# Fixing every engine's order by a table, splitting the first matmul groups by contraction halves, pairing k-v products and moving casts to ScalarE in a fused attention and feed-forward kernel

## The chip, the cores and the metric

The kernel runs on one core of one Trainium2 chip. The metric is device time in microseconds (us) of one execution, lower is better. The profile's span is about 1.8 us shorter than that time (308.2 us of span for a run of 310.04 us before). Engines: PE = TensorE, DVE = VectorE, ACT = ScalarE, POOL = GpSimd, SP = SyncE.

## The reference, cut to what matters

```python
# attention without a sequence-by-sequence product: q, k, v are (8, 8, 576, 64)
q_s = softmax(q, axis=-1)                      # over the 64 channels
k_s = softmax(k, axis=2)                       # over the 576 positions
kv  = einsum('bhsd,bhse->bhde', k_s, v)        # a 64x64 matrix per head
attn = einsum('bhsd,bhde->bhse', q_s, kv)
# feed-forward on x = (4608, 512): 512 -> 2048 -> 512
h = x @ w_in
g = where(h > 0, h, exp(min(h, 0)) - 1)
out = g @ w_out
```

The kernel works in 16 units of attention (two per batch; a unit n is four heads of a batch) and nine blocks of 512 tokens of feed-forward. GEMM1 is `x @ w_in`, GEMM2 is `g @ w_out`; each is 576 matmuls of 128 x 128 weights by 512 columns in fp32r (4 bytes a number: W1's 512 x 2048 come in eight transfers of 512 KB). In a block GEMM1 has eight groups of eight matmuls, counted from 0. In the names of the profiles W is a weight, QR, KR and VR are the loaded q, k and v, QS is q divided by its sums, VB is v in bf16, MBLK is the scaled k-v product, XT is the attention's result X (the x of GEMM1), ESB is the activation's buffer, GT is g, PS is PSUM and OSB the buffer of a finished tile.

## The kernel before

All work is described as a list of operations with an engine, a modelled duration and the buffers read and written. A scheduler then walks the list with a model of the machine and picks, for each engine, what to issue next. Semaphore waits follow from the buffers.

```python
def order(self):                      # the kernel before
    seq = self.one_pass({})           # greedy: the earliest ready operation, ties by key
    for _ in range(8):
        seq = self.one_pass(self.fluid(seq))   # again with modelled DMA landings
    return self.fill(seq)             # dummy matmuls in PE's modelled gaps at the start
```

The start of the program, which the argument is mostly about:

```python
for n, t in ((0, "q"), (1, "q"), (0, "k"), (0, "v"), (1, "k"), (1, "v")):
    self.load(n, t, -40, "sp", ...)           # 590 KB each, on SP's queue
    if (n, t) == (0, "v"): gate = S.ops[-1]
for s in range(4):                            # W1 by quarters of its columns, on POOL's queue
    self.load_w1(s, -30, [gate] if s == 0 else ())
# ... exp(q), exp(k) on ACT; V to bf16 on POOL; q sums and q/sum (QS) on DVE;
# ... q transposed by PE (side 'tp'), k-v product (kv_mm), X = kv applied to q (ao_mm), X evicted (xt)
self.side(0, -3, self.kv_mm(1, 0))
S.spare_until = S.ops[-1]                     # dummy matmuls stop here
```

A group of GEMM1 (`hg`) and what its result goes through, and the store of a finished tile:

```python
for t in range(2):
    for kc in range(4):                       # all four contraction chunks of W1 and X
        e.matmul(P[:, t*512:(t+1)*512], W1[:, kc, ...], XT[:, kc, ...], start=(kc==0), stop=(kc==3))
# ACT: esb = exp(P);  DVE: esb = min(esb,1)-1;  DVE: GT = max(esb, P)
...
S.add("act", ..., lambda e: e.activation(osb, bank, AF.Copy))         # out_store
for x in range(2):
    S.add("sp", ..., lambda e: e.dma_start(rows[b, c], osb[x*64:(x+1)*64, :]))
```

The softmax here doesn't subtract the row's maximum and nothing guards it: scores larger than these inputs give would overflow.

Of the kernel before, what the change touches and what calls it, by code (L numbers as in the profile page):

```python
# [19 lines left out]
ISSUE = {"sp": 620, "act": 650, "gp": 760}  # L20


class Op:
    __slots__ = ("eng", "dur", "emit", "deps", "key", "idx", "start", "end",
                 "dma", "sem", "val", "clock", "nbytes", "follow", "side", "late", "packet", "margin",
                 "gate")

    def __init__(self, eng, dur, emit, key, dma=None, nbytes=0):
        self.eng, self.dur, self.emit, self.key = eng, dur, emit, key
        self.deps = {}  # L30
        self.dma, self.nbytes = dma, nbytes
        self.start = self.end = None
        self.follow, self.side, self.packet, self.margin = None, 0, 4608, 0


class Sched:
# [3 lines left out]
    HOP = 90  # L40
    SLACK = 60
    LATE = 200
    SPIN_FROM = 3000.0
    DMA_LAT = 1650
    FIRST = {"sp": 1650, "act": 1650, "gp": 2300}
    DMA_RATE = 375.0
# [37 lines left out]
    def order(self):  # L84
        seq = self.one_pass({})
        for _ in range(8):
            seq = self.one_pass(self.fluid(seq))
        return self.fill(seq)

    def fill(self, seq):  # L90

        out, free, done = [], self.SPIN_FROM, False
        for o in seq:
            if o.eng == "pe" and not done:
                idle = o.start - free - 150
                count = int(36 + (idle - 3600) / 57 if free == self.SPIN_FROM else idle / 57)
                if count > 0:
                    p = Op("pe", count * 57, self.spare(count), 0)
                    p.start, p.end = free, free + p.dur
                    p.deps = {d: "raw" for d in self.spare_after}  # L100
                    out.append(p)
                free = o.end
                done = o is self.spare_until
            out.append(o)
        return out

    def fluid(self, seq):

        queues = {}
        for o in seq:  # L110
            if o.dma:
                queues.setdefault(o.eng, []).append([o.start + self.FIRST[o.eng], float(o.nbytes), o])
        t, land = 0.0, {}
        while any(queues.values()):
            live = [q[0] for q in queues.values() if q and q[0][0] <= t]
            coming = [q[0][0] for q in queues.values() if q and q[0][0] > t]
            if not live:
                t = min(coming)
                continue
            share = {id(x): self.DMA_RATE * x[2].packet / sum(y[2].packet for y in live)  # L120
                     for x in live}
            step = min([x[1] / share[id(x)] for x in live] + [c - t for c in coming])
            t += step
            for x in live:
                x[1] -= share[id(x)] * step
                if x[1] < 1:
                    land[x[2]] = t + 200 + x[2].margin
            for e in queues:
                queues[e] = [x for x in queues[e] if x[2] not in land]
        return land  # L130

    def one_pass(self, land):
        for o in self.ops:
            o.start = o.end = None
        queues = {e: [o for o in self.ops if o.eng == e] for e in self.ENG}
        free = {e: 0.0 for e in self.ENG}
        out, used = [], [0, -1, -2]
        left = len(self.ops)

        def ready(o):  # L140
            t = 0.0
            if o.follow is not None and o.follow.start is None:
                return None
            if o.gate is not None:
                if o.gate.start is None:
                    return None
                t = o.gate.start
            for d in o.deps:
                if d.end is None:
                    return None  # L150
                hop = self.HOP if d.eng != o.eng or d.dma else 0 if o.eng == "pe" else 40
                t = max(t, d.end + hop)
            return t

        while left:
            best = None
            for e in self.ENG:
                q = queues[e]
                if not q:
                    continue  # L160
                heads = q
                if e == "pe":
                    heads = [next((o for o in q if o.side == x), None) for x in (0, 1, 2)]
                    heads = [o for o in heads if o is not None]
                can = []
                for o in heads:
                    t = ready(o)
                    if t is not None:
                        if e == "pe" and o.side and o.late:
                            t += self.LATE  # L170
                        order = (used[o.side], o.idx) if e == "pe" else (o.key, o.idx)
                        can.append((max(t, free[e]), order, o))
                if not can:
                    continue
                first = min(c[0] for c in can)
                slack = 60 if e == "pe" else self.SLACK
                s, _, o = min((c for c in can if c[0] <= first + slack), key=lambda c: c[1])
                pick = (None, o, s)
                if pick and (best is None or pick[2] < best[2]):
                    best = (e, pick[1], pick[2])  # L180
            e, o, s = best
            queues[e].remove(o)
            if e == "pe":
                used[o.side] = s
            o.start = s
            free[e] = s + o.dur
            o.end = s + o.dur
            if o.dma:
                o.end = max(s + self.DMA_LAT + o.nbytes / self.DMA_RATE, land.get(o, 0))
            out.append(o)  # L190
            left -= 1
# [52 lines left out]
def t_act(n, psum):  # L244
    return n / 1.2 + (90 if psum else 105)


def t_dve(n, fast=1):
    return n / 0.96 / fast + 75


def t_f32r(n):
    return (n + 33) / 2.4


class Gen:
# [49 lines left out]
    def init(self):  # L306
# [4 lines left out]
            pattern=[[-1, 128]], channel_multiplier=1), -38, X=["ID"])  # L311
        S.add("dve", 60, lambda e: e.memset(self.RZK[0][:, :], 0.0), -90, W=["RZK0"])
        S.add("act", 1400, lambda e: e.activation(self.RZK[0][:, :], self.RZK[0][:, :], AF.Exp), -80,
              X=["RZK0"])
        for i in range(2):
# [5 lines left out]
    def load(self, n, t, key, eng="gp", follow=None):  # L321
# [9 lines left out]
        S.ops[-1].margin = 300 if n < 4 else 1500 if n < 6 else 5000  # L331
# [9 lines left out]
    def load_w1(self, s, key, after=()):  # L341
        w = self.w_in.rearrange("(h kc d) f -> h d kc f", h=2, d=D)
        sl = slice(s * 512, (s + 1) * 512)
        for h in range(2):
            self.S.add("gp", ISSUE["gp"], lambda e, h=h: e.dma_start(
                self.W1[h:128:2, :, sl], w[h, :, :, sl]), key,
                W=[f"W1_{s}{h}"], dma=f"w1{s}{h}", nbytes=1 << 19, after=after, follow=self.gpq)
            self.gpq = self.S.ops[-1]
        return self.gpq
# [9 lines left out]
    def stage1(self, n, key, vconv="gp"):  # L359
# [5 lines left out]
        S.add("act", t_act(1152, False), lambda e: e.activation(flat(q), flat(q), AF.Exp),  # L365
              key - 3, X=[f"qR{i}"])
        ek = self.ek(i)
        S.add("act", t_act(1152, False), lambda e: e.activation(  # L368
            ek[:, :, :, :].rearrange("p h c d -> p (h c d)"), flat(k), AF.Exp),
            key - 2, X=[f"kR{i}"])  # L370
        hs = slice(0, 2) if vconv == "gp" else slice(0, 1)
        eng, t = ("gp", 1250) if vconv == "gp" else ("dve", t_dve(576) + 60)
        S.add(eng, t, lambda e: e.tensor_copy(  # L373
            VB[:, hs, :, 0:D], v[:, hs, :, :]), key - 50, R=[vname], W=[f"VB{i}"])
        self.conv = S.ops[-1]
        if vconv != "gp":
            S.add("act", t_act(576, False), lambda e: e.activation(
                VB[:, 1:2, :, 0:D], v[:, 1:2, :, :], AF.Copy), key - 50, R=[vname],
                W=[f"VB{i}x"])
            self.conv2 = S.ops[-1]  # L380
        S.add("dve", t_dve(1152) + 60, lambda e: e.tensor_reduce(  # L381
# [3 lines left out]
        S.add("dve", 250, lambda e: e.reciprocal(self.RZQ[i][:, :, :], self.ZQ[i][:, :, :]),  # L385
# [3 lines left out]
        S.add("dve", t_dve(1152) + 60, lambda e: e.tensor_tensor(  # L389
# [8 lines left out]
    def tp(self, n, ps, key, engs=("act", "act"), after=()):  # L398
# [7 lines left out]
        for (c0, c1, at, X, W), eng in zip(cuts, engs):  # L406
# [7 lines left out]
            S.add("pe", (c1 - c0) * 56 + 60, mm, key, R=[f"QS{self.alt(n)}", "ID"], X=X, side=1)  # L414
# [6 lines left out]
            else:  # L421
                S.add("dve", t_dve(n_) + 60, lambda e, dst=dst, src=src: e.tensor_copy(dst, src),
                      key, W=W, X=X, after=after)

    def turn(self, n, key):

        i, qs = n % 2, self.QS[self.alt(n)]
        self.S.add("sp", ISSUE["sp"], lambda e: e.dma_start_transpose(
            self.QT[:, :, :], qs[:, :, :].rearrange("p c t -> p (c t)")),
            key - 60, R=[f"QS{self.alt(n)}"], W=["QT"], dma="tq", nbytes=128 * 2304)  # L430
        self.S.ops[-1].packet, self.S.ops[-1].margin = 512, 5000

    def widen(self, n, key):
        i, T = n % 2, self.qsT[self.alt(n)]
        self.S.add("gp", 1200, lambda e: e.tensor_copy(  # L435
            T[:, :, :].rearrange("p c t -> p (c t)"),
            self.QT[:, :, :].rearrange("p c t -> p (c t)")),
# [378 lines left out]
```

## Time and profile before

Three runs before the prediction had a median of 308.61 us (307.98 to 308.88). What matters:

| quantity | value | read from |
|---|---|---|
| 512-column matmuls | 1152, 1.81 us per eight, 261.2 us | PE timeline |
| first GEMM1 matmul | 16.91 us | PE timeline |
| last matmul ends | 304.30 us | chain of waits |
| stalls between 38 and 82 us | about 3.9 us, an estimate | PE timeline, start to start |
| W1's first two transfers land | 15.30 and 16.66 us | the trace's landings |

From the page of the kernel before: the span, each engine's busy time, PE's granted clock in 40 slices, and the chain of work that ended last.

```profile
span 308.2 us, 4602 instructions
PE 296.4 (96%) x1938; PEld 241.9 (78%) x1938; DVE 201.6 (65%) x244; ACT 161.9 (53%) x190; POOL 55.3 (18%) x54
...
PEclk9979999999999999999999999999999999999999
...
PE 87%; DMA 4%; DVE 4%; ACT 2%; issue 1%; POOL 1%; SPq 0%
```

PE is the chain for 87% of the span, so a gain can only come from its gaps, its clock or less work for it. The one digit 7 in the clock row is a cold stretch. The windows view of the kernel before shows it: each row is a stretch in us, its length, each engine's busy us (with instructions), the granted clock, the DMA share and GB/s.

```profile
14.00:17.00 3.00, 1.49 (x31) 1.07 (x15) 1.83 (x6) 2.00 (x5) 3.00 (x6) 0.99 1.11 331
17.00:20.00 3.00, 3.00 (x7) 2.34 (x8) 0.00 (x0) 0.00 (x0) 3.00 (x5) 0.50 1.19 373
38.00:50.00 12.00, 11.29 (x132) 8.76 (x131) 7.64 (x12) 6.36 (x8) 5.05 (x8) 1.00 1.12 374
60.00:70.00 10.00, 8.20 (x76) 6.10 (x75) 9.66 (x15) 8.12 (x10) 1.15 (x1) 1.00 0.83 255
100.00:110.00 10.00, 10.00 (x80) 8.23 (x79) 8.79 (x11) 4.79 (x7) 2.47 (x2) 1.00 0.72 236
```

From 17 to 20 us PE is "busy" all the time at half the clock: busy time alone hides it. From 60 to 70 us PE is idle for 1.8 us while DVE and ACT are both over 80% busy. At 100 us PE has no gap left. The waits of PE in the kernel before (us in total, times, longest), without some that end before 16 us. Of the 2.2 us in the first line, 1.7 end at 9.08 us, at the start, and 0.55 at 39.62:

```profile
PE PS L412 <- DVE QS L389: 2.2, 2, 1.7
...
PE PS L545 <- DMA W<-in_moe_w_in_dram: 1.0, 1, 1.0
PE PS L545 <- DVE GT L573: 0.8, 1, 0.8
PE PS L545 <- DVE GT L567: 0.7, 2, 0.4
PE PS L491 <- ACT XT L513: 0.6, 1, 0.6
```

The timeline of the start (start us, length us, engine, line, operation, and what ended the idle time before it) shows who started when:

```profile
9.77 1.15 POOL L373 CAST VB<-VR 128x1152 bf16<-128x1152 f32 x1 [8.31 <-DMA VR<-in_v_dram]
10.62 1.51 DVE L389 TENSOR_TENSOR QS<-QR,RZQ 128x1152 f16<-128x1152 f32 x1
10.86 5.08 POOL L345 DMA_DIRECT2D W<-in_moe_w_in_dram  x8
```

POOL casts unit 0's V first and issues W1's transfers after it. And the end of the same kernel in the timeline:

```profile
304.32 0.60 ACT L600 ACTIVATE OSB<-PS 128x512 f32<-128x512 f32 x1 [3.03 <-PE PS L583]
304.94 1.11 SPq L609 DMA_DIRECT2D out_dram<-OSB  x2
```

After the last eviction SP issues two half stores one after the other.

### The profile page before, as it was taken

Reading aid. Unit: us, or ns where it says so; the run is one execution under the profiler, and the core shown is the slowest. Engines: PE = TensorE matmul, PEld = TensorE weight load, DVE = VectorE, ACT = ScalarE, POOL = GpSimd, SP = SyncE. Lnnn points to the kernel's source line nnn. Section 1 sums busy time; section 2 is a strip of 40 time slices with the busy share of each in tenths; the row PEclk is TensorE's granted clock in tenths of the full one; section 3 lists DMA queues with packets and bytes.
Section 4 is the critical chain, followed back from the end, with each engine's and each line's share of the span. In section 5 each row is a group of like instructions: output and inputs, shape, how many; then the busy total and the mean of one; then the engine's idle time right before and its main releaser. Section 6 shows DMA issues by size and latency. Waiting matters only on the chain.

```text
span 308.2 us, 4602 instructions
## 1 busy us (share of the span) xinstructions
PE 296.4 (96%) x1938; PEld 241.9 (78%) x1938; DVE 201.6 (65%) x244; ACT 161.9 (53%) x190; POOL 55.3 (18%) x54
## 2 busy tenths in 40 slices
PE   7789999989999999999999999999999999999994
PEld 7567777668788888888888888888888888888783
DVE  3927874798897959595959596866544445555500
ACT  4738756979685546464646463734343443333311
POOL 0790144111211115050404040301000000000000
PEclk9979999999999999999999999999999999999999
DMA  7999999887778766566665654031111221111122
GB/s 263 312 361 389 390 389 323 273 264 136 242 186 228 260 157 187 150 186 149 183 150 159 168 169 87 21 78 30 34 36 39 46 47 41 34 34 34 36 68 68
DMA packets 33429, 49.39 MB, mean 160 GB/s; under 512 B 13952, under 2 KB 13952, under 8 KB 33408
## 3 DMA queue, kind: packets, MB, share of 16 engines
q1 hardware_dynamic: 27392, 33.63, 39.7%
q0 software_dynamic: 6016, 15.47, 16.0%
q8 instruction: 15, 0.25, 0.3%
q14 instruction: 6, 0.05, 0.1%
HBM read 36.70 MB, written 9.44 MB: 150 GB/s over the span
## 4 chain that ended last, share of the span: by engine, by line
PE 87%; DMA 4%; DVE 4%; ACT 2%; issue 1%; POOL 1%; SPq 0%
PE PS L545 42%; PE PS L583 41%; DMA VR<-in_v_dram 2%; PE PS L491 2%; DMA W<-in_moe_w_in_dram 2%; PE PS L461 2%; DVE QS L389 1%; ACT ESB L554 1%; DVE ZQ L381 1%; DVE GT L567 1%; ACT ESB L565 1%; SPq L329 0%; DVE GT L573 0%; PE PS L412 0%; POOL VB L373 0%
## 5 line engine op out<-in xcount | busy, mean ns | idle before, releaser
L545 PE MATMUL PS<-XT,W 128*128 128x512 f32 x576 | 144.0, 394 | 2.5 <-DMA W<-in_moe_w_in_dram 1.0
L583 PE MATMUL PS<-W,GT 128*128 128x512 f32 x576 | 144.9, 393 | 0.0
L545 PEld LDWEIGHTS PS<-XT,W 128*128 128x128 f32 x576 | 108.6, 190 | 26.9 <-DVE GT L567 1.8
L554 ACT ACTIVATE ESB<-PS 128x1024 f32<-128x1024 f32 x72 | 73.9, 1027 | 95.3 <-PE PS L545 95.2
L583 PEld LDWEIGHTS PS<-W,GT 128*128 128x128 f32 x576 | 106.1, 188 | 22.0 <-DVE GT L573 0.5
L571 DVE TENSOR_SCALAR ESB<-ESB 128x1024 f32<-128x1024 f32 x64 | 52.0, 813 | 68.0 <-ACT ESB L554 67.6
L573 DVE TENSOR_TENSOR GT<-ESB,PS 128x1024 fp32r<-128x1024 f32 x64 | 78.1, 1221 | 2.2
L600 ACT ACTIVATE OSB<-PS 128x512 f32<-128x512 f32 x32 | 19.2, 599 | 35.1 <-PE PS L583 35.1
L435 POOL CAST qsT<-QT 128x1152 fp32r<-128x1152 f16 x10 | 18.4, 1843 | 95.6 <-PE PS L461 91.7
L373 POOL CAST VB<-VR 128x1152 bf16<-128x1152 f32 x15 | 20.0, 1335 | 56.2 <-DMA VR<-in_v_dram 56.2
L381 DVE TENSOR_REDUCE ZQ<-QR 128x18 f32<-128x1152 f32 x16 | 21.6, 1349 | 6.3 <-ACT QR L365 6.2
L389 DVE TENSOR_TENSOR QS<-QR,RZQ 128x1152 f16<-128x1152 f32 x16 | 23.6, 1477 | 0.5
L513 ACT ACTIVATE XT<-PS 128x640 fp32r<-128x640 f32 (+5 forms) x32 | 19.7, 618 | 3.0 <-PE PS L491 2.8
L365 ACT ACTIVATE QR<-QR 128x1152 f32<-128x1152 f32 x16 | 18.6, 1165 | 2.9 <-DMA QR<-in_q_dram 2.9
L368 ACT ACTIVATE KR<-KR 128x1152 bf16<-128x1152 f32 x16 | 18.6, 1161 | 1.6 <-DMA KR<-in_k_dram 1.6
L491 PE MATMUL PS<-qsT,MBLK 128*128 128x320 f32 (+3 forms) x64 | 14.2, 306 | 1.1 <-ACT XT L513 0.6
L491 PEld LDWEIGHTS PS<-qsT,MBLK 128*128 128x128 f32 x64 | 11.6, 189 | 4.5 <-DVE MBLK L474 1.0
L567 DVE SCALAR_TENSOR_TENSOR GT<-PS,ESB 128x1024 fp32r<-128x1024 f32 x8 | 9.8, 1222 | 6.0 <-ACT ESB L565 6.0
L474 DVE TENSOR_TENSOR MBLK<-PS,RZK 64x128 fp32r<-64x128 f32 x32 | 9.3, 289 | 1.1
L648 PE MATMUL PS<-ID 128*128 128x128 f16 x92 | 8.4, 269 | 1.5 <-POOL ID L309 1.5
L648 PEld LDWEIGHTS PS<-ID 128*128 128x128 f16 x92 | 7.7, 126 | 1.7 <-POOL ID L309 1.5
L565 ACT ACTIVATE ESB<-ESB 128x1024 f32<-128x1024 f32 x8 | 8.5, 1061 | 0.1
(28 smaller groups left out, 61.0 us busy)
## 6 DMA issues: line engine op xcount, KB each, us to landing
out_dram<-OSB SPq DMA_DIRECT2D x64, 128.0 KB, 2.4
QR<-in_q_dram SPq DMA_DIRECT2D x12, 576.0 KB, 4.8
KR<-in_k_dram SPq DMA_DIRECT2D x12, 576.0 KB, 4.7
VR<-in_v_dram SPq DMA_DIRECT2D x12, 576.0 KB, 5.0
W<-in_moe_w_in_dram POOLq DMA_DIRECT2D x8, 512.0 KB, 7.8
W<-in_moe_w_out_dram POOLq DMA_DIRECT2D x4, 1024.0 KB, 18.2
QR<-in_q_dram POOLq DMA_DIRECT2D x4, 576.0 KB, 12.7
KR<-in_k_dram POOLq DMA_DIRECT2D x4, 576.0 KB, 13.0
```

The lines of the kernel that those rows point to most:

```text
L365: S.add("act", t_act(1152, False), lambda e: e.activation(flat(q), flat(q), AF.Exp), key - 3, X=[f"qR{i}"])
L373: S.add(eng, t, lambda e: e.tensor_copy(VB[:, hs, :, 0:D], v[:, hs, :, :]), key - 50, R=[vname], W=[f"VB{i}"])
L381: S.add("dve", t_dve(1152) + 60, lambda e: e.tensor_reduce(self.ZQ[i][:, :, :].rearrange("p h c -> p (h c)"), q[:, :, :, :].rearrange("p h ...
L389: S.add("dve", t_dve(1152) + 60, lambda e: e.tensor_tensor(qso, q[:, :, :, :], rz, ALU.mult), key - 3, R=[f"qR{i}", f"RZQ{i}"], W=[f"QS{se ...
L491: last = e.matmul(P[:, f * 512:f * 512 + n_], M[:, f, :], T[:, c0:c1, f * 64:f * 64 + 64], start=True, stop=True)
L513: S.add("act", t_act((h1 - h0) * n_, True), lambda e, dst=dst, src=src: e.activation(dst, src, AF.Copy), key, W=W, X=X)
L545: last = e.matmul(P[:, t * 512:(t + 1) * 512], self.W1[:, kc, tt * 128:(tt + 1) * 128], self.XT[:, kc, rc:rc + BLK], start=(kc == 0), stop ...
L554: S.add("act", t_act(1024, True), lambda e: e.activation(esb[:, :], P[:, :], AF.Exp), key, W=[f"E{i}"], X=banks)
L571: S.add("dve", t_dve(1024, 2) + 80, lambda e: e.tensor_scalar(esb[:, :], esb[:, :], 1.0, -1.0, ALU.min, ALU.add), key, X=[f"E{i}"])
L573: S.add("dve", t_dve(1024) + 90, lambda e: e.tensor_tensor(gt, esb[:, :], P[:, :], ALU.max), key, R=[f"E{i}"], W=gw, X=banks)
L583: last = e.matmul(dst, GT[:, jj, ts * 128:(ts + 1) * 128], self.W2[:, jj, :], start=(jj == 0), stop=(jj == 15))
L600: S.add("act", t_act(512, True), lambda e: e.activation(osb[:, :], src, AF.Copy), key, W=[f"O{i}0", f"O{i}1"], X=[f"b{bk}"])
```

## The change

Its intent: replace the greedy order by one that was searched for off the chip, with better modelled durations; let the first GEMM1 groups start when half of the contraction is there; give PE fewer separate k-v products; and take the late casts away from POOL. The core of the diff (the table has 805 operation numbers; durations of the model and plumbing are cut):

```diff
+CASTS = 6
+ORDER = {
+    "pe": ("26 30 28 44 40 42 47 64 51 65 67 68 66 69 79 ... "),
+    "act": ("3 20 31 21 22 32 27 29 41 45 52 70 ... "),
+    "dve": (...), "gp": ("1 14 15 16 17 18 33 19 54 ... "),
+    "sp": ("8 9 10 11 12 13 179 ... 796 792 800 803 799 "),
+}
 def order(self):
-    seq = self.one_pass({})
-    for _ in range(8):
-        seq = self.one_pass(self.fluid(seq))
-    return self.fill(seq)
+    line = {e: [self.ops[int(i)] for i in ORDER[e].split()] for e in self.ENG}
+    ...                                   # times are modelled, the order is the table's
+    SPIN_FROM = 9400.0                    # dummy matmuls from 9.4 us on; before: from the start
-        for s in range(4):
-            self.load_w1(s, -30, [gate] if s == 0 else ())
+        for two, half in ((0, 0), (0, 1), (1, None)):     # columns 0-1023 by contraction halves
+            self.load_w1(two, half, -30, [gate, self.ident] if (two, half) == (0, 0) else ())
-        self.stage1(0, -8)
+        self.stage1(0, -8, vconv="act")                   # unit 0's V is cast on ACT
+        for half in range(2):
+            for g in range(3):
+                self.hg_mm(0, g, turns[g], key, half)     # groups 0 to 2: two matmul halves each
...
-            at(use + 2, ao(n, 1, n + 1 if n + 1 < NU else None), loads(("k", n + 3)))
+            pair = n > 6 and n % 2 and n + 1 < NU
+            at(use + 2, ao(n, 1, (n + 1, n + 2) if pair else (5,) if n == 4 else ()))
...
 def widen(self, n, key):                                 # q cast; V casts likewise
+    if n < CASTS: ... "gp" ...
+    else: self.S.add("act", ..., lambda e: e.activation(dst, src, AF.Copy), ...)
...
-            S.add("sp", ISSUE["sp"], lambda e, ...: e.dma_start(rows[b, c], ...))
+            q = "act" if x and gi == 8 * NBLK - 1 else "sp"   # the very last half store
+            S.add(q, ISSUE[q], lambda e, ...: e.dma_start(rows[b, c], ...))
```

## The prediction

> **What bounds the kernel now.** The tensor engine. The chain that ended last is 87% PE, 83% of it the two GEMMs. Eight 512-column matmuls take 1.81 us start to start in the timeline, so 1152 need 261.2 us of the 308.2 us span. From 90 us on, the windows show PE busy 10.00 of every 10 us; the change can win there only by giving PE less to do.
>
> What is not GEMM, from the PE timeline:
> - Start: the first GEMM1 matmul is at 16.91 us; PE waited the last 0.98 us for W1. The first W1 transfer was issued at 10.86 us, behind POOL's cast of V (9.77 to 10.92 us).
> - Cold clock: PEclk is 0.50 from about 17 to 20.3 us; the first 64 matmuls take 16.41 us instead of 14.51, a loss of 1.9 us. [...]
> - Stalls between 38 and 82 us (QS, X evictions, GT): about 3.9 us of start-to-start excess.
> - Attention pieces: a lone k-v product costs about 0.41 us, plus 0.14 us on the matmuls after it.
> - Tail: after the last matmul (304.3 us), an eviction of 0.60 us, two stores issued one after the other by SP, landing at 308.2 us.
>
> **What the change does.**
> 1. Casting the first V on ScalarE frees POOL, so W1 is issued at about 9.8 us. Its first megabyte took from about 13.4 to 16.67 us; now it should land at about 15.4. As one contraction half of eight tiles it lets the first groups start with only unit 0's X. The second half lands about 2.7 us later, so PE waits briefly again; group 3 should end near 23.7 us, against 26.1. Gain about 2.3 us, warm clock included; 1 us less if the clock drops anyway. That stays open: dummy matmuls still stop after the second k-v product.
> 2. The fixed order should remove half to two thirds of the 3.9 us of stalls, not all: DMA runs at about 390 GB/s to 40 us, so units 2 and 3 can't arrive much earlier, and DVE and ACT are each over 80% busy from 60 to 80 us. [...] after 90 us ACT has that room (3 to 6.5 us busy of 10), around 72 to 90 us hardly. Gain about 2.2 us.
> 3. Five k-v pairs: the second product saves its own start and switch, 0.25 to 0.3 us. Gain 1.3 us. POOL's freed 38 us are off the chain.
> 4. The last half store on ACT's queue: about 0.45 us.
> 5. Cost: four 64-column products and two more evictions, about 0.35 us.
>
> Sum: 2.3 + 2.2 + 1.3 + 0.45 - 0.35 = 5.9 us.
>
> **Prediction.** 302.6 us, range 299.8 to 305.3. Faster by over 2% (under 302.4 us): 0.5; within 2%: 0.49; slower: 0.01.
>
> **What would show the steps.** First GEMM1 matmul near 15.5 us, PEclk without a 0.5 slice after it, group 3 ending before 24.5 us; idle of PE between 38 and 90 us under 2 us; two units in about 30.9 us instead of 31.5 after 120 us; 3.5 us from last matmul to end; POOL empty late, ACT busier.
>
> **What would make it wrong.** The clock dropping at the first groups; W1's second half or W2 arriving late, giving the early start back at 24 or 40 us; a table fitted to modelled times that puts an engine in order behind a late DMA; casts delaying exponentials. Faster than told, about 300 us, if nearly all stalls go.

The forecast's sum is 5.9 us. Cut are a sentence on what sets off the cold clock, which no run shows, and the time that the kernel's model gives a cast on ScalarE, so "that room" is room for these casts. In the traces ACT takes 1.16 us for its instructions of that size, 128 x 1152 (page of before, L365 and L368), and the 21 casts of the changed kernel took 1.16 us each, 24.5 us in all (its page, L366 and L430). Two figures of the forecast are estimates: the second half's 2.7 us is 1 MB at the 390 GB/s of before (windows view, 24 to 40 us), and the saving of a k-v pair is my reading of the 0.41 and 0.14 us of a lone product.

## The result, and the profile after

The changed kernel took 305.6 us (305.46 to 305.82, 4 runs) against 308.75 us (307.98 to 309.24, 4 runs). The ratio is 0.9901, with a 95% interval of 0.9879 to 0.9923. Ratios here are the mean time of one kernel's fast runs over that of the other's of the same rounds, so they are not quite the ratio of the medians. Repeated later, the same kernel gave 0.9881 (0.9847 to 0.9916). The gain is about 3 to 3.7 us, not 5.9.

The same views as before, now of the changed kernel. The page:

```profile
span 303.7 us, 4456 instructions
PE 289.2 (95%) x1875; PEld 235.6 (78%) x1875; DVE 189.2 (62%) x243; ACT 180.5 (59%) x210; POOL 21.6 (7%) x32
...
PEclk9999999999999999999999999999999999999999
...
PE 90%; DMA 5%; DVE 1%; POOL 1%; ACT 1%; SPq 0%; issue 0%
```

The cold slice is gone, POOL's work fell from 55.3 to 21.6 us and ACT's grew by 18.6 us. DMA has a larger share of the chain than before: a first hint. The windows:

```profile
14.00:17.00 3.00, 2.00 (x50) 1.31 (x48) 2.49 (x4) 1.19 (x2) 3.00 (x5) 1.00 0.94 289
17.00:20.00 3.00, 2.91 (x12) 2.10 (x13) 1.34 (x4) 0.60 (x1) 3.00 (x5) 1.00 1.12 411
38.00:50.00 12.00, 12.00 (x135) 9.30 (x134) 5.15 (x10) 7.68 (x10) 5.62 (x7) 1.00 0.99 331
60.00:70.00 10.00, 10.00 (x86) 7.85 (x85) 8.61 (x13) 9.42 (x11) 0.00 (x0) 1.00 0.61 183
```

The stalls between 38 and 82 us are gone. All of PE's waits in the changed kernel:

```profile
PE PS L402 <- DVE QS L379: 9.6, 2, 9.2
PE PS L541 <- ACT XT L507: 0.6, 1, 0.6
```

In the first line, 9.2 us are the wait before any work could start. The timeline of the start:

```profile
9.31 1.17 ACT L366 ACTIVATE VB<-VR 128x1152 bf16<-128x1152 f32 x1 [0.34 <-DMA VR<-in_v_dram]
9.59 3.24 POOL L334 DMA_DIRECT2D W<-in_moe_w_in_dram  x5 [8.14 <-DMA VR<-in_v_dram]
12.61 2.60 DVE L379 TENSOR_TENSOR QS<-QR,RZQ 128x1152 f16<-128x1152 f32 x1
12.80 1.19 POOL L363 CAST VB<-VR 128x1152 bf16<-128x1152 f32 x1
17.00 1.19 PE L541 MATMUL PS<-XT,W 128*128 128x512 f32 x4 [0.65 <-ACT XT L507]
```

W1 is issued 1.27 us earlier, as meant, and yet the first GEMM1 matmul comes at 17.00 us instead of 16.91. The chain of work in the changed kernel, up to 36 us (start, length, what):

```profile
9.59 1.97 POOL W L334 x3
11.56 8.05 DMA W<-in_moe_w_in_dram
19.61 0.04 issue
19.65 13.27 PE PS L541 x56
```

It runs through the landing of W1's second half at 19.61 us, not through PE. But PE stood for it only about 0.25 us (the matmul before started at 19.17 us and takes 0.23), and W1's last piece lands at 25.33 us, just before group 4 starts at 25.37. A second profile of the same kernel names another path (number 5). And the end:

```profile
299.63 0.60 ACT L603 ACTIVATE OSB<-PS 128x512 f32<-128x512 f32 x1 [2.47 <-PE PS L586]
300.25 1.11 SPq L613 DMA_DIRECT2D out_dram<-OSB  x2
300.26 0.54 ACTq L613 DMA_DIRECT2D out_dram<-OSB  x1
```

There are still two stores on SP after the last eviction, and one on ACT besides.

Cut in three, the two profiled spans compare so. The middle begins where the 64 matmuls of block 0's GEMM1 are through (33.32 us before, 32.77 after) and ends at the last matmul (304.30 and 299.61); both middles hold 1088 of the large matmuls:

| part | before | after | won | predicted |
|---|---|---|---|---|
| start, to the 64th GEMM1 matmul | 33.32 | 32.77 | 0.55 | 2.3 |
| middle | 270.98 | 266.84 | 4.14 | 3.15 (2.2 + 1.3 - 0.35) |
| tail, last matmul to the end of the span | 3.94 | 4.08 | -0.14 | 0.45 |
| sum | 308.24 | 303.69 | 4.55 | 5.9 |

The kernel before with 18 more dummy matmuls kept its clock (0.999) in the profile of number 2: its parts are 32.63, 270.32 and 3.94 us. Against these the changed kernel loses 0.14 us at the start, wins 3.49 in the middle and loses 0.14 in the tail, 3.2 us in all.

The prediction failed at the start and at the tail. A third error is not in the table: the span of 308.24 us belongs to a run of 310.04 us, 1.3 us over the median of the timed runs. The experiments are about these three, and about what won the middle.

### The profile page after: what moved, and what is told of

Read it like the earlier page. It is cut to its first block, busy times and chain, and to the rows that moved or that the text cites. A ratio compares the mean times of both kernels' runs of the same rounds, so it can differ in the third digit from the quotient of the medians.

```text
span 303.7 us, 4456 instructions
## 1 busy us (share of the span) xinstructions
PE 289.2 (95%) x1875; PEld 235.6 (78%) x1875; DVE 189.2 (62%) x243; ACT 180.5 (59%) x210; POOL 21.6 (7%) x32
## 3 DMA queue, kind: packets, MB, share of 16 engines
q0 software_dynamic: 4960, 15.47, 15.4%
## 4 chain that ended last, share of the span: by engine, by line
PE 90%; DMA 5%; DVE 1%; POOL 1%; ACT 1%; SPq 0%; issue 0%
PE PS L541 43%; PE PS L586 42%; PE PS L485 3%; DMA W<-in_moe_w_in_dram 3%; DMA VR<-in_v_dram 2%; PE PS L454 2%; PE PS L402 1%; POOL W L334 1%; SPq L316 0%; DVE QS L379 0%; DVE GT L576 0%; ACT ESB L557 0%; DVE MBLK L467 0%; DVE ESB L574 0%; ACT OSB L603 0%
## 5 line engine op out<-in xcount | busy, mean ns | idle before, releaser
L541 PE MATMUL PS<-XT,W 128*128 128x512 f32 x576 | 141.1, 393 | 0.8 <-ACT XT L507 0.6
L586 PE MATMUL PS<-W,GT 128*128 128x512 f32 x576 | 140.6, 392 | 0.0
L574 DVE TENSOR_SCALAR ESB<-ESB 128x1024 f32<-128x1024 f32 x64 | 44.0, 688 | 66.7 <-ACT ESB L557 66.6
L371 DVE TENSOR_REDUCE ZQ<-QR 128x18 f32<-128x1152 f32 x16 | 21.6, 1348 | 11.0 <-ACT QR L355 11.0
L507 ACT ACTIVATE XT<-PS 128x512 fp32r<-128x512 f32 (+6 forms) x32 | 19.4, 609 | 10.8 <-PE PS L485 10.6
L485 PE MATMUL PS<-qsT,MBLK 128*128 128x320 f32 (+5 forms) x64 | 14.3, 310 | 0.0
L402 PE MATMUL PS<-ID,QS 128*128 128x128 f16 x54 | 4.7, 235 | 9.6 <-DVE QS L379 9.6
L366 ACT ACTIVATE VB<-VR 128x1152 bf16<-128x1152 f32 x11 | 12.8, 1163 | 0.3 <-DMA VR<-in_v_dram 0.3
L430 ACT ACTIVATE qsT<-QT 128x1152 fp32r<-128x1152 f16 x10 | 11.7, 1166 | 1.7 <-PE PS L454 1.7
L402 PEld LDWEIGHTS PS<-ID,QS 128*128 128x128 f16 x54 | 3.3, 104 | 11.2 <-DVE QS L379 10.0
L463 DVE RECIPROCAL RZK<-PS 128x2 f32<-128x2 f32 x16 | 2.6, 164 | 9.9 <-ACT XT L507 5.3
## 6 DMA issues: line engine op xcount, KB each, us to landing
W<-in_moe_w_out_dram POOLq DMA_DIRECT2D x4, 1024.0 KB, 14.5
```

Of the source, the lines that this page charges most:

```text
L371: S.add("dve", t_dve(1152), lambda e: e.tensor_reduce(self.ZQ[i][:, :, :].rearrange("p h c -> p (h c)"), q[:, :, :, :].rearrange("p h c d ...
L485: last = e.matmul(P[:, y:y + n_], M[:, f, :], T[:, c0:c1, f * 64:f * 64 + 64], start=True, stop=True)
L507: S.add("act", t_act((h1 - h0) * n_, True), lambda e, dst=dst, src=src: e.activation(dst, src, AF.Copy), key, W=W, X=X)
L541: last = e.matmul(P[:, t * 512:(t + 1) * 512], self.W1[:, kc, tt * 128:(tt + 1) * 128], self.XT[:, kc, rc:rc + BLK], start=(kc == 0), stop ...
L574: S.add("dve", t_dve(1024, 2), lambda e: e.tensor_scalar(esb[:, :], esb[:, :], 1.0, -1.0, ALU.min, ALU.add), key, X=[f"E{i}"])
L586: last = e.matmul(dst, GT[:, jj, ts * 128:(ts + 1) * 128], self.W2[:, jj, :], start=(jj == 0), stop=(jj == 15))
```

## The experiments

Every experiment was correct against the reference and ran in the same rounds as the kernel before. Where a text compares with the changed kernel, that is 305.6 us (first result) or 305.97 us (its repeat below). The first four, and each later set of four, shared a chip and 11 runs of the kernel before; medians of before were 309.51, 309.23 and 308.95 us.

### 1. The changed operations in the greedy order

```diff
 # on the changed kernel
-ORDER = { ... }                       # and its order()
+    order, one_pass, fluid, fill and their constants as in the kernel before
```

> All the operations of the changed kernel (W1 halves, k-v pairs, casts on ScalarE, last store on ACT), but ordered by the greedy scheduler of the kernel before instead of the table. Theory 'the table is worth most of what was won after 33 us': about 307.3 us, with 2 us or more of PE stalls between 33 and 90 us that the changed kernel does not have. Rival 'the changed operations did it, the table is a detail': 305.6 us, within 0.4 us of the changed kernel. k-v pairs should keep their 1.35 us either way.

Measured: 309.85 us, ratio to before 1.0013 (0.9983 to 1.0044). Without the table nothing at all is won, less than either theory said. All six runs kept the clock (0.998 or more), so they should be set against the runs of before at full clock, 308.45 us (number 2): 1.4 us are lost. PE's waits in this run, those not at the start:

```profile
PE PS L603 <- DVE GT L593: 1.6, 1, 1.6
...
PE PS L558 <- DVE GT L593: 1.4, 1, 1.4
PE PS L603 <- DVE GT L587: 0.8, 1, 0.8
```

These are waits for the results of GEMM1 to pass through ACT and DVE. The middle, counted as above and with the 0.36 us of attention products that came earlier here, took 271.5 us: 0.5 us more than before and 4.7 us more than with the table, although the k-v pairs were there too. In this order the k-v pairs and the casts win nothing in time. The keys by which the greedy scheduler ranks operations were not fitted anew to the changed operations, so this tells what the table does against this greedy order, not against every one. The other side of it: in all ten profiles of kernels that have the table and the casts on ACT the middle takes 266.6 to 267.2 us. The run also shows that the last store on ACT's queue works: from the last matmul (303.88 us) to the end of the span (307.45) there are 3.57 us here, against 3.94 before.

### 2. The kernel before, kept warm

```diff
 # on the kernel before: 18 dummy matmuls into a free PSUM bank just before the first GEMM1 matmul
+            if o is self.first_hg:
+                p = Op("pe", 18 * 57, self.spare(18, 3), 0)
```

> The kernel before with 18 more dummy matmuls between the last X product of the start and the first GEMM1 matmul, where PE waited 0.98 us for W1, so that the clock is not halved afterwards. Theory 'the 1.9 us cold stretch in the profiled run of before is in most of its runs': 306.9 us, that is 1.5 to 1.9 us under the kernel before. Rival 'the profiled run was unlucky, the timed runs seldom have it': within 0.4 us of the kernel before, and the granted clock of most runs of before is above 0.993.

Measured: 308.62 us, ratio 0.9975 (0.9945 to 1.0004), 0.8 us by the means: between the two theories, and the interval just includes no gain at all. Two of its six runs still lost the clock (0.994 and 0.993). In its profile the clock held (1.00 from 13.01 to 19.83 us by the windows view), but W1's second transfer landed at 17.48 us instead of 16.66, so GEMM1 began at 17.73 us and part of the warm clock's worth was gone.

The runs of the kernel before settle the size better. Over the three sets there are 32 fast ones. In 24 the granted clock is 0.995 or less; they average 309.60 us. In 8 it is above; they average 308.45 us and none is over 308.88. So the cold stretch is in three runs of four and costs 1.15 us there, not the 1.9 us that the trace showed at the place itself. On average it costs 0.86 us. The changed kernel's 9 runs all have 0.997 or more.

### 3. The X eviction before the q eviction on ScalarE

```diff
 # on the changed kernel, ACT row of the table
-"3 20 31 21 22 32 27 29 41 45 52 "
+"3 20 31 21 22 32 27 29 45 41 52 "
```

> The changed kernel with two entries of the ScalarE row of the table exchanged: unit 0's X eviction goes before unit 1's q eviction, for which ScalarE stood waiting 2.69 us. First GEMM1 matmul at about 16.0 us instead of 17.0 in both theories. Theory 'the landing of W1's second half at 19.6 us paces the first groups': time within 0.3 us of the changed kernel. Rival 'the order of ScalarE paces them': 0.8 to 1.0 us faster.

Measured: 305.59 us, the same as the changed kernel. The first GEMM1 matmul moved to 16.47 us and nothing came of it; the profile has PE waiting 0.36 us for W1's last transfer at group 4 instead. That it is W1 was the theory, though the last piece (landed at 25.50 us) and not the second half held PE. The order of ScalarE is ruled out as the only pace; number 5 shows that it is a second one, nearly as late.

### 4. W1 issued 1.1 us earlier

```diff
 # on the changed kernel
-            if (n, t) == (0, "v"):
+            if (n, t) == (0, "k"):
                 gate = S.ops[-1]
```

> The changed kernel with W1's first transfer waiting for unit 0's k (landed at 7.78 us) instead of its v (9.29 us). Theory 'W1 paces the start': W1's first half lands about 15 us and its second about 18.3 instead of 15.91 and 19.61, k and v of unit 1 land up to 1 us later; as unit 1's X is ready only 0.2 us before W1's second half, the gain is 0 to 0.4 us. Rival 'W1 alone paces the start': 1.0 to 1.4 us faster.

Measured: 304.34 us, ratio to before 0.9836 (0.9808 to 0.9863), 1.25 us under the changed kernel. That is my rival theory, "W1 alone paces the start"; I had expected 0 to 0.4. My error was to think that unit 1's k and v would be delayed and would be next: v landed at 12.68 us against 12.28 in the changed kernel, but unit 0's k was as much later in this profile (8.17 against 7.78), and W1 was issued after that. W1's first half came only 0.34 us earlier than in the changed kernel, its second half 1.48 us. The landings of W1's transfers, from the traces (in the changed kernels the first two are the first contraction half of 1024 columns, the next two the second half, the last two the other 1024 columns; before, each is half of 512 columns):

```
kernel                         issued   lands, us: 1     2     3     4     5     6
before                         10.86          15.30 16.66 18.94 20.28 21.62 22.97
changed                         9.59          13.93 15.91 18.32 19.61 22.75 25.33
changed, again                 10.17          14.61 15.91 18.27 19.55 22.96 25.53
W1 early                        8.47          14.28 15.57 16.85 18.13 21.32 23.74
three edits of order (no. 8)    8.24          14.50 15.78 17.06 18.34 21.32 23.88
```

Transfers of 0.5 MB (all but the changed kernels' last two, which are 1 MB) follow one another by about 1.3 us where they flow. In the ten profiles where W1 is issued at 9.4 us or later, the third comes 1.6 to 2.7 us after the second. In the four where it is issued by 8.5 us, while SP's loads still run (unit 1's v lands at 12.68 us in this run), there is no such gap (1.28 to 1.29 us). In the gap the transfers are slowed, not stopped: by the windows view 256 GB/s from 14.5 to 16.5 us in the changed kernel, and 289 from 14 to 17 us, where it is 408 with the early W1. The cause of the gap is open; what the earlier landing does for the start is shown by number 8 beside number 3.

### 5. The changed kernel again

> The changed kernel unaltered, so that it shares its chip and its runs of the kernel before with the experiments: 305.6 us, granted clock 0.997 to 1.0 in every run, spread under 0.6 us. Against before on this chip 0.987 to 0.990: the kernel before varies by 3 us from run to run with its clock, so the ratio depends on how many of its runs lost their clock.

Measured: 305.97 us (305.29 to 306.06), ratio 0.9881, clock 0.998 to 1.0 in all five fast runs. As expected. Its profile, however, has another chain at the start. It doesn't pass through W1 but through DVE's q product of unit 1, its transposition, its eviction on ACT and, behind that, unit 0's X eviction (two of its pieces):

```profile
12.91 2.90 DVE QS L379
...
17.59 1.20 PE PS L541 x4
```

W1's second half landed at 19.55 us, and PE came to it at 20.20. The profiles of numbers 6, 7 and 9 have the same chain, with the product at 2.33 to 2.90 us; in all four W1's last piece lands 0.06 to 0.27 us before group 4 starts. So two paths end nearly together in the changed kernel, and shortening one alone can win little.

### 6. Unit 1's V cast behind the last W1 transfer

In the run with the early W1 a second thing had differed. In the changed kernel DVE's q product of unit 1 (QS) takes 2.60 us while POOL's cast of V takes 1.19; there it was the other way round. Timeline of the run with the early W1:

```profile
12.73 1.36 DVE L379 TENSOR_TENSOR QS<-QR,RZQ 128x1152 f16<-128x1152 f32 x1
12.73 2.36 POOL L363 CAST VB<-VR 128x1152 bf16<-128x1152 f32 x1 [1.01 <-DMA VR<-in_v_dram]
```

```diff
 # on the changed kernel, POOL row of the table
-"1 14 15 16 17 18 33 19 54 "
+"1 14 15 16 17 18 19 33 54 "
```

> The changed kernel with two entries of the GpSimd row exchanged: its cast of unit 1's V goes behind the last W1 transfer, about 0.6 us later; W1's first transfer still waits for unit 0's V. It separates two things that were both different in the run with the early W1: there VectorE's q product of unit 1 took 1.36 us and the cast 2.36, here and in the changed kernel they took 2.60 and 1.19. Theory 'the q product held up by the cast sets the start': product 1.3 to 1.4 us, first GEMM1 matmul about 16 us, 0.8 to 1.2 us faster than the changed kernel. Rival 'W1's landing sets it': W1's second half still lands at 19 to 19.6 us, time within 0.4 us of the changed kernel.

Measured: 305.41 us, 0.4 us under the changed kernel by the means of the same rounds, so at the edge of what the rival allowed. But the experiment did not do its job: the cast moved to 13.96 us and the product still took 2.31 us, so the two theories were not told apart by it. Number 8 does that.

### 7. The late casts back on GpSimd

```diff
 # on the changed kernel; the 20 operation numbers move from the ACT row to the end of the POOL row
-CASTS = 6
+CASTS = 16
```

> The changed kernel with the 20 late casts of V and q back on GpSimd, all other rows of the table as they are. Theory of the prediction 'GpSimd's work is off the chain, moving it wins nothing': within 0.4 us of the changed kernel. Rival 'casts on GpSimd hold up VectorE's two-input products and its other work, and their 2.3 us come too late': 0.8 us or more slower, with PE waits on the q casts or on the X evictions after 80 us.

Measured: 306.65 us. Two of its six runs lost the clock (0.991 and 0.992); the other four average 306.50 us, 0.66 us over the changed kernel's 305.84 of the same rounds (all six: 1.1 us). That lies between the two theories. In the profile the middle takes 267.48 us, against 266.83 and 267.01 in the two profiles of the changed kernel. The prediction had said that POOL's late work was off the chain. The timeline shows how it gets on it: POOL's cast, then DVE, then PE, in the order in which they run:

```profile
102.48 1.15 POOL L420 CAST qsT<-QT 128x1152 fp32r<-128x1152 f16 x1 [6.79 <-PE PS L446]
...
102.54 1.64 DVE L566 TENSOR_SCALAR ESB<-ESB 128x1024 f32<-128x1024 f32 x1 [1.68 <-ACT ESB L549]
104.10 1.34 DVE L371 TENSOR_TENSOR QS<-QR,RZQ 128x1152 f16<-128x1152 f32 x1
105.37 1.21 DVE L568 TENSOR_TENSOR GT<-ESB,PS 128x1024 fp32r<-128x1024 f32 x1
...
106.63 1.66 PE L533 MATMUL PS<-XT,W 128*128 128x512 f32 x6 [0.39 <-DVE GT L568]
```

DVE's first step of the activation, 0.69 us elsewhere, took 1.64 us beside the cast, GT came late, and PE waited. That is 0.95 us added to a DVE instruction beside a cast of 1.15 us. The kernel before shows the same: nine of its 64 such steps began while POOL was casting q, and these took 1.31 to 1.64 us, the others 0.68 to 0.70 (timelines of DVE and POOL; POOL's q casts there took 1.15 or 2.26 to 2.33 us, the 2.3 us of the expectation). In the changed kernel, without these casts, their mean is 0.69 us. By what mechanism the two engines hold each other up is not shown. The other rows of the table had been searched without these casts on POOL, so 0.66 us is their worth in this order only.

### 8. Three edits of order together

```diff
 # on the changed kernel
-            if (n, t) == (0, "v"):                 # W1's gate
+            if (n, t) == (0, "k"):
-"... 27 29 41 45 52 "                              # ACT row
+"... 27 29 45 41 52 "
-"... 792 800 803 799 "                             # SP row, its end
+"... 792 800 799 803 "
```

> Three edits of order on the changed kernel together: W1's first transfer waits for unit 0's k, unit 0's X eviction goes before unit 1's q eviction on ScalarE, and the last-but-one tile's second half store goes before the last tile's store on SP (now it is issued after it, at 300.8 us). The early W1 alone gave 304.34 us. Theory 'with W1 early, X evictions pace the start': another 0.2 to 0.6 us from the eviction, and 0.2 to 0.4 us at the tail, so 303.6 us. Rival 'the second q transposition and unit 1's k-v product pace it': 304.1 us.

Measured: 304.06 us (303.89 to 304.17), ratio to before 0.9825 (0.9792 to 0.9859). It beats both kernels: 304.05 us against 305.84 by the means of the same rounds. And it separates in part what number 6 could not: here the q product of unit 1 took 2.35 us and the cast 1.15, as in the changed kernel, yet W1's halves landed at 15.78 and 18.34 us and the gain stayed. Number 3 has the same exchange of evictions and a stretched product too (2.65 us), and differs at the start by W1's gate alone: its 64th matmul was through at 32.94 us, here it is at 31.90. So once the exchange has taken the product off unit 0's path, W1's landing sets the start. What W1 early does with the product stretched and without the exchange is not shown: in number 4's profile the product took 1.36 us. The exchange added nothing to number 4: 31.90 us for the 64th matmul, against 31.53 there, with the unstretched product. What came on top is the tail, 3.64 us from last matmul to end instead of 4.08.

### 9. The tail alone

```diff
 # on the changed kernel, SP row of the table, its end
-"... 792 800 803 799 "
+"... 792 800 799 803 "
```

> The changed kernel with one edit: in the SP row the last-but-one tile's second half store is issued before the last tile's first half, not after it. Theory 'ScalarE's queue would have given the predicted 0.45 us, but this entry takes it back': from the last eviction's start to the end of the span 3.6 us instead of 4.06, median 0.3 to 0.45 us below the changed kernel (305.5 if that is 305.97 here). Rival 'the end is set by the landing of the store, not by who issues it': no difference beyond 0.15 us.

Measured: 305.19 us; the times alone do not separate this from the changed kernel (0.9878 and 0.9881 against before, on different chips). The trace does. Its end:

```profile
299.66 0.60 ACT L603 ACTIVATE OSB<-PS 128x512 f32<-128x512 f32 x1 [2.47 <-PE PS L586]
300.29 0.47 SPq L613 DMA_DIRECT2D out_dram<-OSB  x1
300.29 0.54 ACTq L613 DMA_DIRECT2D out_dram<-OSB  x1
```

One store on each queue; from the last matmul (299.64 us) to the end of the span (303.27) 3.63 us instead of 4.08, 0.45 us. In the table of the change the half store of the tile before stood last in SP's row, behind the store that waits for the last eviction. It was ready long before and was issued last, at 300.76 us.

### 10. The split of the first groups undone

```diff
 # on the changed kernel: a half group waits for both contraction halves of W1, and goes behind unit 1's X product
-        ws = [... for x in sorted({kc // 2 for kc in kcs}) for h in range(2)]
+        ws = [... for x in range(2) for h in range(2)]
-"26 30 28 44 40 42 47 64 51 65 67 68 66 69 79 "
+"26 30 28 44 40 42 47 51 64 67 65 68 66 69 79 "
```

> The changed kernel with the split of the first three GEMM1 groups undone in effect: each of their first halves waits for both contraction halves of W1. Theory 'the split lets PE work while W1's second half arrives': the first GEMM1 matmul at 19.6 us instead of 17.0, the 64th ends about 1.5 us later, and the time is 1.3 to 1.6 us above the changed kernel. Rival 'the start is not on the chain, later stages absorb it': within 0.4 us.

Measured: 308.56 us, 2.6 to 3 us over the changed kernel, twice what the theory said. The windows view of this run tells why:

```profile
14.00:17.00 3.00, 2.09 (x52) 1.45 (x50) 2.52 (x2) 0.63 (x2) 3.00 (x5) 1.00 0.99 309
17.00:20.00 3.00, 1.40 (x3) 0.68 (x4) 1.62 (x5) 0.94 (x3) 3.00 (x5) 0.62 1.09 403
20.00:23.00 3.00, 3.00 (x8) 2.35 (x9) 0.31 (x1) 0.22 (x1) 1.71 (x3) 0.50 1.12 414
```

Until W1's second half is there PE waits (1.39 us for DVE's MBLK, then 0.24 us for W1), the clock drops (0.62 and 0.50 in the rows above), and 64 matmuls take 17.01 us instead of 14.51. Five of the six runs have a clock of 0.994 or less. The one run that kept it (0.998) took 306.64 us, the five average 308.93. So the split is worth roughly 0.7 to 1 us by the matmuls done while W1 arrives, which rests on one run, and 2.3 us by the clock, which all nine runs of the changed kernel kept at 0.997 or more. The place of the first groups in PE's row was changed with the wait, and the two were not tried apart.

### 11. A warm start

```diff
 # on the changed kernel, with W1's gate on unit 0's k and the mended SP row
-    SPIN_FROM = 9400.0
+    SPIN_FROM = 3000.0                # 80 dummy matmuls from 1.5 us on
```

> The changed kernel with W1's first transfer waiting for unit 0's k, the SP row mended, and about 80 dummy matmuls from 1.5 us on as the kernel before had them, so that PE is at full clock before unit 0's products. W1 early alone gave 304.34 us, with the mended SP row and the exchanged eviction 304.06. Theory 'with W1 early PE's own cold pieces pace the start' (unit 0's X product takes 1.3 us cold, 0.5 warm): first GEMM1 matmul at 15.2 us, 303.3 to 303.6 us. Rival 'W1's last quarter, landing near 23.8 us, paces it now': 303.9 to 304.1 us.

Measured: 304.30 us, no better than the three edits. Neither number of the expectation holds well; the theory of PE's cold pieces falls. Unit 0's X product did take 0.58 us, to the start of the next, instead of 1.31 (0.36 us of which were a wait for DVE). That PE's pieces are slower in the changed kernel's start is seen in their lengths, for its record of the clock begins only at 14.46 us: nine dummy matmuls took 1.17 us there and 0.67 here, unit 0's k-v product 0.71 and 0.48. PE then waited 1.63 us for W1's first half, which landed at 16.84 us in the profiled run, the slowest of the six. Three of the six runs lost the clock (0.993, 0.993, 0.994).

### 12. W1 before unit 0's k

```diff
 # on the kernel of number 11
-            if (n, t) == (0, "k"):
+            if (n, t) == (1, "q"):
                 gate = S.ops[-1]
```

> As the run with the warm start, but W1's first transfer waits only for unit 1's q (about 6.3 us), so its packets compete with the loads of k and v. Theory 'bytes pace the start: 5.6 MB at 390 GB/s can't be there before 17 us': W1's second half lands at 17.0 to 17.5 us, k and v of unit 1 up to 1 us later, time within 0.3 us of the run with the warm start. Rival 'W1 wins and the attention inputs lose': 0.5 us or more slower, with PE waiting for unit 0's or 1's k-v product.

Measured: 306.42 us, 2.1 us slower than number 11: the rival. The rate in the expectation is the 390 GB/s of before (windows view, 24 to 40 us), and its 17 us an estimate from it. W1's transfers ran beside unit 1's v, which landed at 15.64 us instead of 12.54. POOL's cast began at 15.69 us instead of 12.60, PE waited 1.6 us for it before unit 1's k-v product, and W1's second half still landed only at 18.73 us. All six runs lost the clock (0.989 to 0.994); how much of the 2.1 us this makes is not shown. The two profiles can't be set against each other, because number 11's is of a slow run that had lost it too.

## Why the prediction was wrong, point by point

The measured 305.6 us lies 0.3 us outside the range of 299.8 to 305.3 and 3.0 us over the 302.6 us that I gave.

1. **Start: "Gain about 2.3 us, warm clock included". This step failed.** The profiles show 0.55 us. I had W1's first megabyte landing at 15.4 us, the second at 18.1 and group 3 ending at 23.7. They landed at 15.91 and 19.61 us, W1's last piece at 25.33, and group 3 ended at about 25.4. I had taken the rate of the best stretch, about 390 GB/s, for the whole transfer, though the trace of before already shows 2.28 us between the second and third landing where a free-flowing pair has 1.35. Numbers 4 and 8 show that this is the term: with W1 issued earlier and without the gap the kernel gains 1.25 us, and beside number 3 the 64th matmul comes from 32.94 to 31.90 us by W1 alone. I had also missed a wait that ends nearly as late: the table puts unit 0's X eviction on ACT behind unit 1's q eviction, and this behind DVE's q product, stretched to 2.60 us. So the first GEMM1 matmul came at 17.00 us and not near 15.5. Taking this away alone won nothing (number 3).
2. **The clock inside that step.** The trace of before records 3413 ns at half clock, from 16.94 to 20.35 us. And I charged the full 1.9 us of one profiled run against a median of other runs. By 32 runs of before it is in three of four and worth 1.15 us there, 0.86 us on average. The profile of before was of a run of 310.04 us.
3. **What is left of the start is nothing, or less.** Compare runs at full clock: 308.45 us before and about 305.7 after, 2.75 us. The middle won 4.14 us and the tail lost 0.14, so the new start would be about 1.25 us slower than the old start is when that keeps its clock. This is worked out, not measured, and the size is open. The cut of the profiles gives 1.35 us: 33.32 less the 1.9 us of cold clock is 31.4 us, against 32.77. The one profile of the old start at full clock (number 2) gives only 0.14 us, 32.63 against 32.77, with W1's second transfer 0.8 us late in it; and with its middle of 270.32 us the sum above leaves 0.6 us. The split pays (number 10), but against an order that begins with W1 by contraction halves, not against the old start.
4. **Table: "about 2.2 us" of 3.9 us of stalls. Too low.** The middle won 4.14 us in all, or 3.49 against the profile of number 2; less 1.35 us for the k-v pairs and with 0.36 us of new small products, about 2.5 to 3.15 us of stalls and other gaps went. PE's windows between 38 and 90 us are full. Number 1 shows that, of the two orders tried, only the table's does it.
5. **k-v pairs: "1.3 us". Right in the trace.** A pair takes 0.71 us of PE plus 0.14 after it, two lone ones twice 0.42 plus 0.14: 0.27 us saved, five times. I had it unconditional; in the greedy order nothing of it is left in the time.
6. **"POOL's freed 38 us are off the chain". Wrong by 0.66 us**, in this order (number 7). DVE is the way onto the chain.
7. **Tail: "about 0.45 us". Not delivered.** One entry of the table put an older store last on SP, which cost 0.45 us (number 9). Where that was not so, the tail took 3.57 to 3.64 us against 3.94 before (numbers 1, 8 and 9): 0.3 to 0.37 us, somewhat less than I had said.
8. The check that I had named of "two units in about 30.9 us instead of 31.5" could not be read: the table changed how much GEMM work lies between pairs.

Of the ways to be wrong that I had named, "W1's second half or W2 arriving late" happened with W1. "A table fitted to modelled times that puts an engine in order behind a late DMA" happened in kind, behind late evictions (point 1 and the tail), not behind a DMA.

## What to carry to other kernels

A fixed order can only win where the model behind it has the waits right: first measure the landings of the first transfers one by one, because a rate read from a full stretch of DMA was 1.5 us too hopeful here. Before charging a cold clock or a slow profile to a kernel, look at how many of its timed runs have it. Take the chain of waits from more than one profile: two profiles of this one kernel name two different paths for its start. After any change of queue for a last store, look at what each queue does after the last eviction: an entry standing behind a waiting one costs as much as the store that was moved, 0.45 us here.

## What the runs leave open about the hardware

- What makes the clock drop. In the 3.41 us before each drop (as long as the stretch at half clock itself) PE was busy, by the windows view or PE's timeline, for 1.90 us (before, from 13.53 us), 1.77 (number 10, from 14.32), 1.62 (number 11, from 14.08) and 1.53 (number 12), in pieces; the longest wait of PE near the drop was 0.98, 1.39, 1.63 and 1.65 us. The busy share alone is not the rule: stretches with 1.71 us (before, 6.70 to 10.11), 1.53 (number 2, 6.18 to 9.59) and 1.91 (number 7, 12.24 to 15.66) kept it. What decides is open.
- The gap in W1's transfers from POOL's queue: 0.5 MB each 1.28 us apart when issued by 8.5 us, while SP's loads still ran, but 1.6 to 2.7 us between the second and third in the ten profiles where they were issued 0.9 us or more later. No run here shows its cause.
- Who is held up when DVE and POOL run beside each other. QS and the V cast took 1.36 and 2.36 us (number 4) and 2.35 and 1.15 (number 8); they began within 0.01 us of each other, so these pairs don't tell whether the earlier start decides. In the changed kernel QS began 0.19 us before the cast (12.61 and 12.80 us; 0.47 in its repeat) and was the one held, 2.60 us against 1.19. In number 6 both were long, 2.31 and 2.23 us, with QS begun 1.08 us earlier. This stays open.
